# One contiguous tile of block-diagonal queries, loaded with its zeros in one DMA

## The chip, the cores and the metric

One core of a Trainium2 chip runs the whole program. The metric is device time in microseconds, from the first instruction to the end of the launch. The profile shows one execution of the same program.

## The reference, cut to what matters

A block-sparse attention is followed by two feed-forward layers. The part that the change touches is the scores:

```python
scores_l = scale * np.matmul(q, k.transpose(0, 1, 3, 2))       # masked to |i - j| < 16
k_sum = k.reshape(B, H, nb, 32, D).max(axis=3)                 # 24 blocks of 32 keys
scores_s = scale * np.einsum('bhsd,bhnd->bhsn', q, k_sum) + np.log(32)
a = softmax(concatenate([scores_l_m, scores_s], axis=-1))
x = matmul(a, concatenate([v, v_sum], axis=2))                 # -> (1536, 512)
h = x @ w_in;  x = (h - np.tanh(h)) @ w_out                    # d_ff 2048
xn = x / rms(x) * rms_g
out = (silu(xn @ w_gate) * (xn @ w_val)) @ w_out2              # d_ff 1536
```

There are 2 batches, 8 heads, 768 positions and a head dimension of 64, in float32. The feed-forward weights come as float64 and are split on the chip into pairs of float32r.

## The kernel before, in words

**Attention.** The positions of a batch are cut into six tiles of 128 queries (`TPB`). A unit `u` is one tile with four of the eight heads, so a batch has 12 units (u0 to u11, then u12 to u23). A head has only 64 rows of head dimension, so the 128 rows of TensorE hold two half-tiles of 64 queries at once: the stationary operand is block diagonal, with the first 64 queries in rows 0 to 63 and the second 64 in rows 64 to 127, and zeros in the two other quarters. The moving operand is the key window of both halves, 120 columns: 96 local keys and 24 block maxima.

The queries lie in three buffers `q0` to `q2` (`QB`). A buffer is `[128, 2, 64, 8]`, with the heads innermost, so the stationary operand of one head is every eighth float of the row. `zeros` (L168) clears the two zero quarters of each buffer once at the start, on GpSimd, and `qload` (L240) fills the two others with two DMAs of 64 rows each. `scores` (L258) does four matmuls for a unit (L271), VectorE adds the mask and takes the row extreme (L274), ScalarE takes the exponential (L276), VectorE and GpSimd normalise (L277 to L279). `trans` (L282) transposes the result (L286), and `pv` (L294) multiplies by the values (L303) and writes `xT`. The keys of a batch come in four tiles `kw` (L185). A key tile of the second batch takes the buffer of one of the first batch, when the last unit that reads it is through (u4, u5, u10, u11). `ksum_a` and `ksum_b` (L187 to L200) work out the block maxima and put them into the key tiles; two short matmuls each (L196) stand there with the contiguous tile `sel` as the stationary operand.

**Feed-forward.** `decode_next` (L129) loads a raw piece of a weight (L136, three raw buffers) and decodes it: L144 on ScalarE, L145 to L147 on VectorE, L152 on ScalarE or L150 on VectorE, L153 on GpSimd. The first layer starts while attention runs: an up step (`up1`, L315 to L317, 12 matmuls of 256 columns) and three steps later its down step (L350 to L352). Ten decoded pieces fit beside attention. Eight more get their place when the memory of attention is given back.

**Order.** A plan gives every task a due time (`task`, L428), the tasks are written out in that order, and the language's scheduler then places the instructions on each engine's queue by its own timeline. So an edit can move instructions that it does not touch. All DMAs are issued from one queue (SP), in order, and a DMA there waits until an earlier one has landed, eight places back.

Of the kernel before, what the change touches and what calls it, by code (L numbers as in the profile page):

```python
# [7 lines left out]
F32 = mybir.dt.float32  # L8
# [8 lines left out]
B, H, S, D = 2, 8, 768, 64  # L17
# [7 lines left out]
TPB = S // 128  # L25
KT = TPB // 2
LOC = 64 + 2 * WIN
WID = LOC + NB
# [7 lines left out]
QB = 3  # L36
# [9 lines left out]
DLD = 10  # L46
# [15 lines left out]
PTV = 0  # L62
KBUF = 4
PVS = (1, 1)
TQZ = 0.3
PB = 4
PTB = 3
SHIFT = {}
# [4 lines left out]
TQ = (0.2, 3)  # L73
# [10 lines left out]
def attn_moe_kernel(ctx: ExitStack, tc: tile.TileContext, ins, out, dbg=None):  # L84
    nc = tc.nc
    V, A, G, T = nc.vector, nc.scalar, nc.gpsimd, nc.tensor
# [13 lines left out]
    ap1 = att_ctx.enter_context(tc.tile_pool(name="ap1", bufs=1))  # L100
# [16 lines left out]
        nc.sync.dma_start(out=mask, in_=ins["mask"])  # L117
        nc.sync.dma_start(out=rg, in_=ins["rms_g"])

# [1 line left out]
    pieces = []  # L121
    for m in range(FF1 // 128):
        pieces += [("w_in", m), ("w_out", m)]
# [29 lines left out]
        G.tensor_tensor(w[:, 1], d, f(w[:, 0]), ALU.subtract)  # L153
        wt[name, m] = w

# [1 line left out]
    kwin, kmax, vsum, vt_ = {}, {}, {}, {}  # L157
    p_t, pt_t = {}, {}
    q_b = [ap1.tile([128, 2, 64, 8], F32, name=f"q{i}") for i in range(QB)]
    v_b = [ap1.tile([128, 2, DM], F32, name=f"v{i}") for i in range(VB)]  # L160
    v_of = {}
    xT = cst.tile([128, NT // 128, 2, KD, 128], F32R, name="xT")
# [1 line left out]

    def unit(u):
        return u // (2 * TPB), (u // 2) % TPB, u % 2

    def zeros(i):  # L168
        G.memset(q_b[i][0:64, 1], 0.0)
        G.memset(q_b[i][64:128, 0], 0.0)  # L170

    def ksum_a(b, par, hf):
        if not kwin:
# [65 lines left out]

    def qload(i):  # L240
        b, t = divmod(i, TPB)
        for s in range(2):
            nc.sync.dma_start(out=q_b[i % QB][s * 64:(s + 1) * 64, s].rearrange("p n k -> p (n k)"), in_=ins["q"][b, t, s])

    def vload(i):
        b, t = divmod(i, TPB)
# [3 lines left out]
    def vfill(i):  # L250
        b = i // TPB
        v = v_b[i % VB]
        if v_of.get(i % VB) != b:
            v_of[i % VB] = b
            for s in range(2):
                nc.sync.dma_start(out=v[LOC:WID, s], in_=vsum[b])

    def scores(u):  # L258
        b, t, par = unit(u)
        q = q_b[(u // 2) % QB].rearrange("p s n k -> p (s n) k")  # L260
        kw = kwin[b, par, t // KT][:, t % KT].rearrange("p (j k c) -> p j k c", j=5, k=4)
        mk = mask[:, 1 if 0 < t < TPB - 1 else (0 if t == 0 else 2)]
        P = Pp.tile([128, 4, WID], F32, name="P")
        nb = sp.tile([128, 4], F32, name="nb")
        sm = sp.tile([128, 4], F32, name="sm")
        nh = 2 if (u < S2) != (f"sh{u}" in ALT) else 4
        for k0 in range(0, 4, nh):
            ps = ps_h.tile([128, 512], F32, name="h") if u < SSH else ps_t.tile([128, 512], F32, name="t")
            for i in range(nh):
                k = k0 + i  # L270
                T.matmul(ps[:, i * WID:(i + 1) * WID], q[:, :, 4 * par + k], kw[:, :, k], start=True, stop=True)  # L271
            for i in range(nh):
                k = k0 + i
                V.tensor_tensor_reduce(P[:, k], ps[:, i * WID:(i + 1) * WID], mk, -0.125, 3e38, ALU.add, ALU.min, nb[:, k:k + 1])  # L274
        for k in range(4):
            A.activation(P[:, k], P[:, k], AF.Exp, scale=-1.0, bias=nb[:, k:k + 1], accum_out=sm[:, k:k + 1])  # L276
        V.tensor_scalar(sm, sm, 1e-9, None, ALU.add)  # L277
        V.reciprocal(sm, sm)
        (V if (u < PSV) != (f"ps{u}" in ALT) else G).tensor_tensor(P, P, sm.rearrange("p (k o) -> p k o", o=1).to_broadcast([128, 4, WID]), ALU.mult)  # L279
        p_t[u] = P  # L280

    def trans(u):  # L282
        P = p_t.pop(u)
        ps = ps_t.tile([128, 512], F32, name="t")
        for k in range(4):
            T.transpose(ps[0:WID, k * 128:(k + 1) * 128], P[:, k], ident)  # L286
        pt = ptp.tile([128, 512], F32, name="pt")
        if (u % 4 < PTV) != (f"pt{u}" in ALT):
            V.tensor_copy(pt[0:WID], ps[0:WID])
        else:  # L290
            A.activation(pt[0:WID], ps[0:WID], AF.Copy)
        pt_t[u] = pt
# [13 lines left out]
        A.activation(xh, ov, AF.Copy)  # L306
        V.tensor_tensor(xl, ov, f(xh), ALU.subtract)

# [1 line left out]
    def up(ps, w, t0, t1):  # L310
        o = ps[:, 0:(t1 - t0) * 128]
        for kk in range(KD):
            ws = slice(kk * 128, (kk + 1) * 128)
            xh, xl = xT[:, t0:t1, 0, kk], xT[:, t0:t1, 1, kk]
            T.matmul(o, w[:, 0, ws], xh, start=(kk == 0), stop=False)  # L315
            T.matmul(o, w[:, 1, ws], xh, start=False, stop=False)  # L316
            T.matmul(o, w[:, 0, ws], xl, start=False, stop=(kk == KD - 1))  # L317
# [37 lines left out]
    for md, chunks in enumerate((NCH, NCH2)):  # L355
        m0 = 0
        for j, nch in enumerate(chunks):
            t0 = 0
            pos = 2 * (j == len(chunks) - 1) + (j == 0)
            k = len(chunks) * 0 + (j if md == 0 else len(NCH) + j)  # L360
# [61 lines left out]
            A.activation(xh, pv, AF.Copy, scale=rg[:, kk:kk + 1])  # L422
            V.scalar_tensor_tensor(xl, pv, rg[:, kk:kk + 1], f(xh), ALU.mult, ALU.subtract)

# [1 line left out]
    plan = {}  # L426

    def task(key, at, fn, *req):  # L428
        plan[key] = (at + SHIFT.get(key, 0), len(plan), fn, req)
# [8 lines left out]
    def t_sc(u):  # L438
        u = ORD.index(u) if u < len(ORD) else u
        return TS0 + min(u, UF) * DT0 + max(u - UF, 0) * DT1  # L440

    for i in range(QB):
        task(f"z{i}", TQZ + i, lambda i=i: zeros(i))
    task("sel", TSEL, lambda: nc.sync.dma_start(out=sel, in_=ins["sel"]))
    task("cst", TC, consts)
    for par in range(2):
        at = TK01 * par
# [6 lines left out]
    at = t_sc(2 * TPB)  # L454
    for par in range(2):
        for hf in range(2):
            i = 2 * par + hf + 4 - KBUF
# [5 lines left out]
    for u in range(NU):  # L463
        b, t, par = unit(u)
        at = t_sc(u)
        i = u // 2
        if par == 0:
            task(f"ld{i}", TQ[i] if i < 2 else at - DLD, lambda i=i: qload(i), f"z{i % QB}", *([f"sc{2 * (i - QB) + 1}"] if i >= QB else []))
        task(f"sc{u}", at, lambda u=u: scores(u), f"ld{i}", f"kb{b}{par}", "cst")
        task(f"tr{u}", at + DTR, lambda u=u: trans(u), f"sc{u}")  # L470
        if par == 0:
            task(f"vf{i}", at + DPV - 2, lambda i=i: vfill(i), f"vs{b}", f"vl{i}")
            task(f"vl{i}", TVL[i] if i < 2 else at + DPV - DVL, lambda i=i: vload(i), *([f"pv{i - VB}"] if i >= VB else []))
        if par == 1:
            task(f"pv{i}", at + DPV, lambda i=i: pv(i), f"tr{u - 1}", f"tr{u}", f"vf{i}", *([f"pv{i - 1}"] if i else []))
# [4 lines left out]
    at = TM0  # L480
# [41 lines left out]
def layouts(q, k, v, moe_w_in, moe_w_out, moe2_w_gate, moe2_w_val, moe2_w_out, moe2_rms_g):  # L522
    import numpy as np

    def words(a):
        return np.ascontiguousarray(a).view(np.int64)

    def cols(w):
        n = w.shape[1] // 128
        return np.ascontiguousarray(words(w).reshape(KD, 128, n, 128).transpose(2, 1, 0, 3)).reshape(n, 128, 512)  # L530

    def rows(w):
        return words(w).reshape(w.shape[0] // 128, 128, DM)

    kp = np.zeros((B, H, S + 2 * WIN, D), np.float32)
    kp[:, :, WIN:WIN + S] = k
    vp = np.zeros((B, S + 2 * WIN, DM), np.float32)
    vt = v.transpose(0, 2, 1, 3).reshape(B, S, DM)
    vp[:, WIN:WIN + S] = vt
    order = np.r_[0:72, 80:96, 72:80]  # L540
    rows_at = (64 * np.arange(2 * TPB)[:, None] + order[None, :]).reshape(-1)
    qt = q.reshape(B, 4, 2, TPB, 2, 64, D).transpose(0, 3, 4, 6, 5, 2, 1)
    kw = kp[:, :, rows_at].reshape(B, 4, 2, TPB, 2, 4, 24, D).transpose(0, 2, 4, 7, 3, 5, 1, 6)
    vw = vp[:, rows_at].reshape(B, TPB, 2, LOC, DM).transpose(0, 1, 3, 2, 4)
    vs = v.reshape(B, 4, 2, TPB, 2, 2, BLK, D).transpose(0, 1, 2, 7, 4, 3, 5, 6).reshape(B, 4, 128, S)
    mask = np.zeros((128, 3, WID), np.float32)
    p, c = np.arange(128)[:, None], order[None, :]
    band = (c - p % 64 >= 1) & (c - p % 64 <= 2 * WIN - 1)
    for i in range(3):
        ok = band & ((c >= WIN) | (p >= 64) | (i != 0)) & ((c < 64 + WIN) | (p < 64) | (i != 2))  # L550
        mask[:, i, 0:LOC] = np.where(ok, 0.0, -8e9)
        mask[:, i, LOC:] = 8.0 * np.log(BLK)
    return {
        "q": np.ascontiguousarray(qt).reshape(B, TPB, 2, D, 512),
        "kw": np.ascontiguousarray(kw).reshape(B, 2, 128, TPB, 4 * LOC),
        "vt": np.ascontiguousarray(vs), "vw": np.ascontiguousarray(vw),
        "mask": mask,
        "sel": np.eye(128, dtype=np.float32).reshape(128, 2, 1, 64).repeat(2, axis=2).reshape(128, 256),
        "rms_g": np.ascontiguousarray(moe2_rms_g.reshape(KD, 128).T),
        "w_in": cols(moe_w_in), "w_out": rows(moe_w_out),  # L560
        "w_gate": cols(moe2_w_gate), "w_val": cols(moe2_w_val), "w_out2": rows(moe2_w_out),
    }
# [18 lines left out]
```

## Time and profile before

| | |
|---|---|
| time, three runs | 674.95, 675.65, 677.61 us; median 675.65 |
| span of the profiled execution | 673.4 us, so the median run lies 2.25 us above it |
| TensorE matmuls busy | 650.7 us, 97% |
| TensorE weight loads busy | 545.6 us, 81% |
| VectorE busy | 362.7 us, 54% |
| ScalarE busy | 262.5 us, 39% |
| GpSimd busy | 149.6 us, 22% |
| DMA | 55.71 MB, mean 83 GB/s |

The profile does not show the time of the profiled execution outside its span. PE is TensorE's matmuls, PEld its weight loads, DVE VectorE, ACT ScalarE, POOL GpSimd, SP the queue that issues DMAs. A float32 matmul that is not a transpose shows up as two pairs of a load and a matmul, so a unit of scores has eight records. Attention fills the span up to 142.3 us, with the first feed-forward layer beside it from 41 us on.

### The profile page before, as it was taken

To read this page: it belongs to the slowest core of one execution; us is meant where nothing else is said; L and a number is where in the kernel's file an instruction comes from. 1 tells how busy PE (TensorE), PEld (TensorE's weight loads), DVE (VectorE), ACT (ScalarE), POOL (GpSimd) and SP (SyncE) were. 2 spreads that over 40 slices of the span, in tenths; PEclk is the share of its full clock that TensorE was granted. 3 is DMA by queue.
4 is the path that set the end of the run, shared out by engine and by line. 5 is a ranking of instruction groups with operands and counts; after the bars stand their busy time and mean duration, and the time that the engine had idled before them with its cause. 6 is when DMAs were issued, how large, how long until landed. Compare 5 with 4: busy or idle time off the path is not lost.

```text
span 673.4 us, 8971 instructions
## 1 busy us (share of the span) xinstructions
PE 650.7 (97%) x3336; PEld 545.6 (81%) x3336; DVE 362.7 (54%) x780; ACT 262.5 (39%) x599; POOL 149.6 (22%) x171
## 2 busy tenths in 40 slices
PE   3988999999999999999999999999999999999997
PEld 3977999988778888888888888888888888888886
DVE  4898584469984387626577742222576611311312
ACT  1875775645542345325455332212445311111110
POOL 2558721124320123202052220001233200000000
PEclk9989999999999999999999999999999999999999
DMA  9978362004440024101023310000334000100101
GB/s 288 282 213 244 110 220 66 25 32 157 143 170 1 27 68 155 63 1 62 23 72 114 107 62 1 0 1 0 126 125 152 7 0 1 52 11 1 62 1 62
DMA packets 19827, 55.71 MB, mean 83 GB/s; under 512 B 2360, under 2 KB 5688, under 8 KB 19784
## 3 DMA queue, kind: packets, MB, share of 16 engines
q1 hardware_dynamic: 19784, 55.15, 25.2%
q8 instruction: 26, 0.43, 0.3%
q14 instruction: 17, 0.14, 0.1%
HBM read 51.70 MB, written 3.15 MB: 81 GB/s over the span
## 4 chain that ended last, share of the span: by engine, by line
PE 85%; DVE 8%; DMA 3%; issue 2%; SPq 1%; POOL 0%; ACT 0%; DVEq 0%; ACTq 0%; POOLq 0%
PE h L315 10%; PE h L316 10%; PE h L317 10%; PE acc L350 8%; PE acc L351 8%; PE acc L352 8%; PE t L317 5%; PE t L315 5%; PE t L316 5%; PE t L271 4%; DVE dt L146 2%; PE accx L352 2%; PE accx L351 2%; PE accx L350 2%; DMA kw<-kw 2%
## 5 line engine op out<-in xcount | busy, mean ns | idle before, releaser
L153 POOL TENSOR_TENSOR w<-dt,w 128x512 fp32r<-128x512 f32 x68 | 93.4, 1379 | 289.1 <-ACT w L152 277.0
L315 PE MATMUL h<-xT,w 128*128 128x512 f32 (+1 forms) x384 | 141.5, 369 | 2.1 <-DVE gt L325 2.0
L316 PE MATMUL h<-xT,w 128*128 128x512 f32 (+1 forms) x384 | 140.6, 366 | 0.0
L317 PE MATMUL h<-xT,w 128*128 128x512 f32 (+1 forms) x384 | 140.4, 366 | 0.0
L350 PE MATMUL acc<-w,g 128*128 128x512 f32 x264 | 104.7, 399 | 1.9 <-ACT g L333 1.8
L351 PE MATMUL acc<-w,g 128*128 128x512 f32 x264 | 103.8, 393 | 0.4 <-DVE g L334 0.4
L352 PE MATMUL acc<-w,g 128*128 128x512 f32 x264 | 103.7, 393 | 0.0
L333 ACT ACTIVATE g<-gt 128x512 fp32r<-128x512 f32 (+1 forms) x96 | 55.3, 577 | 112.3 <-DVE gt L345 85.3
L345 DVE TENSOR_TENSOR gt<-t,gt 128x512 f32<-128x512 f32 x36 | 24.8, 690 | 133.0 <-PE t L317 130.0
L315 PEld LDWEIGHTS h<-xT,w 128*128 128x128 f32 x384 | 72.5, 189 | 16.3 <-DVE gt L325 4.0
L316 PEld LDWEIGHTS h<-xT,w 128*128 128x128 f32 x384 | 72.7, 189 | 12.6
L317 PEld LDWEIGHTS h<-xT,w 128*128 128x128 f32 x384 | 72.4, 189 | 12.1
L334 DVE TENSOR_TENSOR g<-gt,g 128x512 fp32r<-128x512 f32 (+1 forms) x96 | 64.5, 673 | 32.7 <-ACT g L333 31.6
L144 ACT ACTIVATE da<-raw 128x512 f32<-128x512 f32 x68 | 45.4, 672 | 64.8 <-DVE dt L146 23.4
L350 PEld LDWEIGHTS acc<-w,g 128*128 128x128 f32 x264 | 49.4, 188 | 12.8 <-ACT g L333 2.1
L351 PEld LDWEIGHTS acc<-w,g 128*128 128x128 f32 x264 | 49.9, 189 | 10.9 <-DVE g L334 0.7
L352 PEld LDWEIGHTS acc<-w,g 128*128 128x128 f32 x264 | 49.6, 188 | 11.0
L147 DVE SCALAR_TENSOR_TENSOR dt<-raw,dt 128x512 uint32<-128x512 uint32 x68 | 57.7, 849 | 1.0
L145 DVE TENSOR_SCALAR dt<-raw 128x512 uint32<-128x512 uint32 x68 | 40.2, 591 | 32.0 <-POOL w L153 30.4
L325 DVE TENSOR_TENSOR gt<-h,gt 128x512 f32<-128x512 f32 (+1 forms) x60 | 34.6, 577 | 41.5 <-ACT gt L324 41.3
L317 PE MATMUL t<-xT,w 128*128 128x512 f32 x144 | 56.5, 392 | 0.0
L315 PE MATMUL t<-xT,w 128*128 128x512 f32 x144 | 56.4, 392 | 0.0
(83 smaller groups left out, 863.7 us busy)
## 6 DMA issues: line engine op xcount, KB each, us to landing
raw<-w_out SPq DMA_DIRECT2D x28, 512.0 KB, 3.3
raw<-w_in SPq DMA_DIRECT2D x16, 512.0 KB, 3.5
raw<-w_gate SPq DMA_DIRECT2D x12, 512.0 KB, 3.6
raw<-w_val SPq DMA_DIRECT2D x12, 512.0 KB, 3.2
kw<-kw SPq DMA_DIRECT2D x8, 576.0 KB, 4.9
v<-vw SPq DMA_DIRECT2D x12, 384.0 KB, 5.7
q<-q SPq DMA_DIRECT2D x24, 128.0 KB, 4.9
out_dram<-part SPq DMA_DIRECT2D x12, 256.0 KB, 2.1
```

The source lines that it names most:

```text
L144: A.activation(a, r[:, :, 1].bitcast(F32), AF.Copy, scale=2.0 ** -112)
L145: V.tensor_scalar(t, r[:, :, 0], 29, None, ALU.logical_shift_right)
L147: V.scalar_tensor_tensor(t, r[:, :, 1], 0x80000000, t, ALU.bitwise_and, ALU.bitwise_or)
L153: G.tensor_tensor(w[:, 1], d, f(w[:, 0]), ALU.subtract)
L315: T.matmul(o, w[:, 0, ws], xh, start=(kk == 0), stop=False)
L316: T.matmul(o, w[:, 1, ws], xh, start=False, stop=False)
L317: T.matmul(o, w[:, 0, ws], xl, start=False, stop=(kk == KD - 1))
L333: A.activation(g[:, 0, 0:n], t[:, 0:n], AF.Copy)
L334: V.tensor_tensor(g[:, 1, 0:n], t[:, 0:n], f(g[:, 0, 0:n]), ALU.subtract)
L350: T.matmul(o, g[:, 0, js], w[:, 0], start=first, stop=False)
L351: T.matmul(o, g[:, 1, js], w[:, 0], start=False, stop=False)
L352: T.matmul(o, g[:, 0, js], w[:, 1], start=False, stop=last)
```

## The change

The query buffer becomes `[128, 8, 128]`: for each head its 128 stationary columns lie side by side, zeros included. The host lays out the input so, with the zero quarters in it, and one DMA of 128 rows by 4 KB loads a tile, where two DMAs of 64 rows by 2 KB did. The GpSimd clears and their tasks are gone. Arithmetic and tile sizes on the chip stay as they were. The input `q` grows from 128 KB twice to 512 KB for a tile.

```diff
-    q_b = [ap1.tile([128, 2, 64, 8], F32, name=f"q{i}") for i in range(QB)]
+    q_b = [ap1.tile([128, 8, 128], F32, name=f"q{i}") for i in range(QB)]
...
-    def zeros(i):
-        G.memset(q_b[i][0:64, 1], 0.0)
-        G.memset(q_b[i][64:128, 0], 0.0)
...
     def qload(i):
         b, t = divmod(i, TPB)
-        for s in range(2):
-            nc.sync.dma_start(out=q_b[i % QB][s * 64:(s + 1) * 64, s].rearrange("p n k -> p (n k)"), in_=ins["q"][b, t, s])
+        nc.sync.dma_start(out=q_b[i % QB].rearrange("p k n -> p (k n)"), in_=ins["q"][b, t])
...
-        q = q_b[(u // 2) % QB].rearrange("p s n k -> p (s n) k")
+        q = q_b[(u // 2) % QB]
...
-                T.matmul(ps[:, i * WID:(i + 1) * WID], q[:, :, 4 * par + k], kw[:, :, k], start=True, stop=True)
+                T.matmul(ps[:, i * WID:(i + 1) * WID], q[:, 4 * par + k], kw[:, :, k], start=True, stop=True)
...
-    qt = q.reshape(B, 4, 2, TPB, 2, 64, D).transpose(0, 3, 4, 6, 5, 2, 1)
+    qt = q.reshape(B, 4, 2, TPB, 2, 64, D).transpose(0, 3, 4, 6, 2, 1, 5).reshape(B, TPB, 2, D, 8, 64)
+    qz = np.zeros((B, TPB, 2, D, 8, 2, 64), np.float32)
+    for s in range(2):
+        qz[:, :, s, :, :, s] = qt[:, :, s]
...
-        "q": np.ascontiguousarray(qt).reshape(B, TPB, 2, D, 512),
+        "q": qz.reshape(B, TPB, 128, 1024),
```

Line numbers of the changed kernel are smaller by 1 to 8. The scores (L271) are L265 there, the transposes (L286) L280, the products with the values (L303) L297, the short matmuls (L196) L191, the up step (L315 to L317) L309 to L311, the decode (L145 to L147) L144 to L146, the normalisation (L277, L278) L271 and L272, L325 is L319, L334 is L328, and L236 is L231.

The scheduler moves instructions on every engine up to about the end of attention; behind it the order is the same. Three places are shown. The first is the DMA queue at the start of the program. Before:

```order
L185 DMA kw<-kw 128x3x384
L243 DMA q_106<-q 64x512 x2
L185 DMA kw<-kw 128x3x384
L444 DMA sel<-sel 128x256
L117 DMA mask<-mask 128x360
```

and now:

```order
L180 DMA kw<-kw 128x3x384
L237 DMA q_106<-q 128x1024
L180 DMA kw<-kw 128x3x384
L436 DMA sel<-sel 128x256
L116 DMA mask<-mask 128x360
```

One DMA stands where two stood, and nothing else moves among the first twelve or so.

The second place is TensorE's queue just ahead of u12, the first unit of the second batch. The short matmuls with `mx` are those of `ksum_b`, `q_106` is the buffer that u12 reads. Before:

```order
L351 MATMUL acc<-w,g 128x512
L352 MATMUL acc<-w,g 128x512
L351 MATMUL acc<-w,g 128x512
L352 MATMUL acc<-w,g 128x512
L196 MATMUL t<-mx,sel 128x48 x2
L271 MATMUL t<-kw,q_106 128x120 x4
L286 MATMUL t<-sel,P 120x128 x4
L315 MATMUL h<-xT,w 128x256 x2
```

and now:

```order
L310 MATMUL h<-xT,w 128x256
L311 MATMUL h<-xT,w 128x256
L309 MATMUL h<-xT,w 128x256
L310 MATMUL h<-xT,w 128x256
L311 MATMUL h<-xT,w 128x256
L191 MATMUL t<-mx,sel 128x48 x2
L265 MATMUL t<-kw,q_106 128x120 x4
L280 MATMUL t<-sel,P 120x128 x4
```

An up step that followed u12 now precedes it: 49 matmuls of 256 columns stand ahead of u12, where 36 stood.

The third place is VectorE's queue between the score reductions of u15 and those of u16. `dt` and `raw` are of the weight decode. Before:

```order
L307 TENSOR_TENSOR xT<-acc,xT 128x512
L334 TENSOR_TENSOR g<-gt,g 128x256
L277 TENSOR_SCALAR sm<-sm 128x4
L278 RECIPROCAL sm<-sm 128x4
L325 TENSOR_TENSOR gt<-h,gt 128x256
L391 COPY part<-acc 128x512
L334 TENSOR_TENSOR g<-gt,g 128x256
L145 TENSOR_SCALAR dt<-raw 128x512
L325 TENSOR_TENSOR gt<-h,gt 128x256
L146 SCALAR_TENSOR_TENSOR dt<-da,dt 128x512
L147 SCALAR_TENSOR_TENSOR dt<-raw,dt 128x512
```

and now:

```order
L328 TENSOR_TENSOR g<-gt,g 128x256
L144 TENSOR_SCALAR dt<-raw 128x512
L145 SCALAR_TENSOR_TENSOR dt<-da,dt 128x512
L144 TENSOR_SCALAR dt<-raw 128x512
L271 TENSOR_SCALAR sm<-sm 128x4
L146 SCALAR_TENSOR_TENSOR dt<-raw,dt 128x512
L272 RECIPROCAL sm<-sm 128x4
L145 SCALAR_TENSOR_TENSOR dt<-da,dt 128x512
L319 TENSOR_TENSOR gt<-h,gt 128x256
L231 TENSOR_SCALAR vsum<-t 24x512
L146 SCALAR_TENSOR_TENSOR dt<-raw,dt 128x512
```

The decode of weight pieces has moved about a unit ahead of the scores. Between the last `ksum_b` copy (L198) and the end of u16, VectorE now has two more decodes of a piece (L145 to L147), the scaling of `vsum` (L236), one more L325 and one more L334. On TensorE, from the first matmul of u12 to the first of u16, there stand 48 matmuls of 256 columns as before, but 16 of 512 columns where there were 7, and four transposes of L224 where there were two.

## Rows read from the trace of the kernel before

**Rows 1.** The page: its first line.

```profile
span 673.4 us, 8971 instructions
```

**Rows 2.** The chain that ended last: start us, us, what.

```profile
54.28 7.09 DMA kw<-kw
...
68.69 0.12 PE h L315
...
127.27 1.90 PE t L271 x8
...
141.15 1.09 PE acc L303 x30
...
142.75 0.63 ACT w L152
...
196.91 0.61 DVE gt L325
```

**Rows 3.** Windows; busy us (instructions) of PE, PEld, DVE, ACT, POOL; clock, DMA share, GB/s.

```profile
14.00:64.90 50.90, 45.46 (x358) 41.77 (x359) 45.16 (x175) 35.27 (x124) 29.48 (x33) 0.97 0.89 258
...
36.00:46.00 10.00, 7.80 (x67) 7.63 (x68) 9.95 (x39) 6.62 (x22) 4.53 (x5) 0.83 0.70 194
...
56.00:66.00 10.00, 8.06 (x66) 6.20 (x64) 8.27 (x29) 5.76 (x16) 7.20 (x11) 1.00 0.89 251
...
64.90:85.80 20.90, 20.90 (x151) 20.23 (x151) 13.60 (x57) 13.86 (x49) 14.84 (x23) 1.00 0.41 133
...
64.90:142.30 77.40, 77.40 (x637) 72.32 (x637) 44.71 (x178) 47.07 (x159) 25.38 (x33) 1.00 0.30 98
...
142.30:200.00 57.70, 54.98 (x267) 44.48 (x268) 54.46 (x77) 31.11 (x59) 22.26 (x16) 1.00 0.40 138
```

**Rows 4.** Line L271: duration in ns (min/median/max), first and last start.

```profile
L271 PEld LDWEIGHTS t<-kw,q x128: 312/335/338, 38.6 to 128.6; 128*128 128x128 f32 x128
...
L271 PE MATMUL t<-kw,q x128: 267/402/498, 38.7 to 128.8; 128*128 128x120 f32 x128
```

**Rows 5.** Line L196, as above.

```profile
L196 PEld LDWEIGHTS t<-mx,sel x16: 186/240/338, 9.1 to 64.8; 128*128 128x128 f32 x16
```

**Rows 6.** Timeline of the weight loads around u12: start us, us, what.

```profile
64.45 0.52 PEld L196 LDWEIGHTS t<-mx,sel 128*128 128x128 f32 x4 [0.75 <-DVE mx L190]
...
64.89 1.98 PEld L271 LDWEIGHTS t<-kw,q 128*128 128x128 f32 x8
```

**Rows 7.** Timeline of TensorE, early; in brackets idle time before, and its releaser.

```profile
19.64 1.06 PE L286 MATMUL t<-sel,P 128*120 128x128 f32 x4
...
20.49 3.89 PE L271 MATMUL h<-kw,q 128*128 128x120 f32 x16
...
24.21 0.60 PE L286 MATMUL t<-sel,P 128*120 128x128 f32 x4
...
28.39 4.04 PE L271 MATMUL h<-kw,q 128*128 128x120 f32 x16 [0.66 <-DMA q<-q]
```

**Rows 8.** Timeline of the DMA queue: the first query load and the fourteenth.

```profile
1.24 1.19 SPq L243 DMA_DIRECT2D q<-q  x2
...
33.68 0.51 SPq L243 DMA_DIRECT2D q<-q  x1
```

**Rows 9.** DMA issues: count, size of each, median us to landing.

```profile
q<-q SPq DMA_DIRECT2D x24, 128.0 KB, 4.9
```

**Rows 10.** VectorE from 64.9 to 142.3 us: busy us, mean ns; idle before.

```profile
L325 DVE TENSOR_TENSOR gt<-h,gt 128x256 f32<-128x256 f32 x15 | 6.3, 417 | 9.4 <-ACT gt L324 9.2
...
L145 DVE TENSOR_SCALAR dt<-raw 128x512 uint32<-128x512 uint32 x5 | 3.1, 617 | 1.6 <-DMA raw<-w_in 1.0 <-DMA raw<-w_out 0.6
...
L146 DVE SCALAR_TENSOR_TENSOR dt<-da,dt 128x512 uint32<-128x512 uint32 x5 | 5.0, 1015 | 0.0
...
L147 DVE SCALAR_TENSOR_TENSOR dt<-raw,dt 128x512 uint32<-128x512 uint32 x5 | 3.5, 695 | 0.0
```

**Rows 11.** Timeline of GpSimd behind its clears.

```profile
10.62 0.34 POOL L199 COPY kw<-kw 128x192 f32<-128x192 f32 x1 [6.56 <-DVE kw L198]
```

More of the change, by code (lines that the diff above doesn't have):

```diff
@@ L64 @@
 PVS = (1, 1)
-TQZ = 0.3
 PB = 4
@@ L440, in t_sc @@
         return TS0 + min(u, UF) * DT0 + max(u - UF, 0) * DT1
-    for i in range(QB):
-        task(f"z{i}", TQZ + i, lambda i=i: zeros(i))
     task("sel", TSEL, lambda: nc.sync.dma_start(out=sel, in_=ins["sel"]))
@@ L467, in attn_moe_kernel @@
         if par == 0:
-            task(f"ld{i}", TQ[i] if i < 2 else at - DLD, lambda i=i: qload(i), f"z{i % QB}", *([f"sc{2 * (i - QB) + 1}"] if i >= QB else []))
+            task(f"ld{i}", TQ[i] if i < 2 else at - DLD, lambda i=i: qload(i), *([f"sc{2 * (i - QB) + 1}"] if i >= QB else []))
         task(f"sc{u}", at, lambda u=u: scores(u), f"ld{i}", f"kb{b}{par}", "cst")
```

## The prediction

> **What bounds the kernel now.** I read the chain of waits first, followed back from the last instruction. Behind 197 us it is TensorE alone. Between 142.75 and 197 us it runs through the decode of weights on VectorE, and that stretch opens when the last `pv` is through and attention gives its memory back: the step ahead of 142.75 is L303 on TensorE at 141.15 [rows 2]. The windows agree: from 142.3 to 200 us VectorE is busy for 54.46 of 57.7 us [rows 3]. So whatever moves the end of attention moves everything behind it, 531.1 us of the 673.4 [rows 1, 3], unchanged in work and in order.
>
> What sets the end of attention I read from the windows ahead of it. From 64.9 to 142.3 us TensorE has no idle time at all (77.40 of 77.40), while VectorE is busy for 44.71 and ScalarE for 47.07 us [rows 3]. That stretch begins with u12, and it is TensorE's. From 14 to 64.9 us no engine alone is the bound: VectorE is busy for 45.16 of 50.9 us, the DMA engines for 0.89 of the time at 258 GB/s, and the chain passes through a key tile that is issued when u11 is through and takes 7.09 us [rows 2, 3].
>
> Then the scores themselves. A unit's eight records take 1.90 us on the chain, 0.237 us each [rows 2]. Is that the matmul or the load of its weights? A matmul of L271 takes 267 ns at the least and 402 in the middle, with the same 120 columns and the same key tile [rows 4]: most of them wait for some 135 ns. The loads take 335 ns [rows 4]. The nearest loads of as many columns from a contiguous tile, L196, take 240 ns in the middle and 186 at the least [rows 5], and four of them stand 0.44 us apart from the next load, 0.110 us each, just ahead of u12 [rows 6]. So it is the load.
>
> **The rule on loads, and the row.** In rows, a load with 32 bytes between columns costs 0.237 us and one without a gap 0.110. The Trainium skill, TensorE: Matmul & The Clock Gate, section LDWEIGHTS (loading the stationary operand), has the time of a load depend on the number of columns alone; by that rule the new layout would load no faster and the sum below would lose its first term. SBUF — State Buffer, section Specifications (TRN2), says that memory is read in lines of 16 bytes and that fewer than two accesses to a line cost bandwidth; by that one the old layout, one float to a line, pays and the new one doesn't. The trace agrees with the second.
>
> **The change, part by part.**
>
> *Faster loads.* From u12 on there are 12 units of eight records, 96 of them. Each falls from 0.237 to 0.110 us if loads still set the pace. Ahead of that there is the matmul itself: its 267 ns against 402 say that it could follow 135 ns sooner, so 0.102 us apart [rows 2, 4], under 0.110. I take 0.127 us for each, 12.2 us. At the lower clock it would be little: the four transposes at 19.64 us take 0.85 us up to the next work, 0.213 each, and 1.06 with their end, those at 24.21 only 0.60 with their end [rows 7]. So TensorE was at the lower of its two levels, 1.2 GHz, up to somewhere between 20.5 and 24.2 us, and I take 22. The sixteen score records at 20.49 cross that point and need 0.233 us each all the same [rows 7]. The strided load does not care for the clock; a contiguous one does.
>
> *Moved matmuls.* Thirteen matmuls of 256 columns now stand ahead of u12 instead of behind it, 0.12 us each [rows 2]: 1.6 us out of the stretch in which TensorE is the bound, into one in which it isn't (8.06 of 10 us busy from 56 to 66 [rows 3], and with faster scores there it has more room). If there is no room they cost the same there, and the term is 0.
>
> *VectorE's decode moved ahead.* Up to the end of u16 VectorE gets two more decodes, 0.617 + 1.015 + 0.695 us each [rows 10], and three more short ones at some 0.42 [rows 10] (for L334 and the scaling of `vsum` that is an estimate from L325): 5.9 us. From 64.9 to 85.8 us, to the end of u16, it is busy for 13.60 [rows 3], so it would need 19.5. TensorE's own work there shrinks by 40 x 0.127 = 5.1 and grows by nine matmuls of 512 columns at 0.24 (an estimate, twice the 256) and two transposes at 0.11: 20.9 - 5.1 + 2.2 + 0.2 = 18.2. VectorE is short by 1.3 us without a gap, and it waits for raw pieces in between. Bounds: 0, if TensorE runs ahead of it by that much, to 5.9. I take 1.6 lost, near the lower end, since units are normalised long before they are transposed. What is late next are the up steps, which wait for VectorE to free the two `h` banks.
>
> *More bytes.* A tile grows by 256 KB. The DMA engines at full share move 258 / 0.89 = 290 GB/s early and 138 / 0.40 = 345 GB/s later [rows 3]: 0.90 or 0.76 us for a tile. Seven tiles are issued by 33.7 us (14 DMAs [rows 8, 9]), so 5.3 to 6.3 us of transfer in a stretch in which the engines have little room. Where it shows is the load that u6 waits for at 28.39 us [rows 7]: four tiles lie up to there, 3.0 to 3.6 us. Against it stand 0.6 us, the issue of a second DMA (two take 1.19 us [rows 8]), saved ahead of the first keys, and about 2 us that TensorE gains from 22 us on (the second half of the sixteen records at 20.49 and the eight behind them, 16 x 0.127). Net I take 0.7 us lost by the start of u12. Bounds: 5.7 lost (6.3 less the 0.6), to 5.7 gained, all that VectorE is idle from 14 to 64.9 us [rows 3]; nothing of it is likely at either end, since VectorE's work up to u12 is the same. Behind 65 us the DMA engines are at 0.30 [rows 3], and the bytes are hidden by that; at a share near 1 they would cost 0.8 us a tile.
>
> *The clears.* Six on GpSimd are gone. They end 6.56 us before GpSimd has its next work at 10.62 [rows 11]; that idle time hides them, and without it they would cost their 3 us.
>
> The sum: -12.2 - 1.6 + 1.6 + 0.7 = -11.5 us. The span goes from 673.4 to 661.9 us, and with the 2.25 us by which the median run lies above the span the time is **664.2 us**, 1.7% less.
>
> **The rivals.**
>
> *The early stage or VectorE takes most of it back.* If the extra bytes delay the raw pieces and the second batch's keys by the full 5, or VectorE's moved decodes cost TensorE their full 5.9 us, the gain is 13.8 less 5 or less 10: 4 to 9 us, 667 to 672. For it: VectorE is at 9.95 of 10 us from 36 to 46 [rows 3], and scores that come sooner don't make it faster. Against it: its idle 7.3 us from 64.9 to 85.8.
>
> *The early stage gives more.* If TensorE's faster scores let u11 finish earlier, the key tile behind it comes earlier and u12 with it, up to the 5.7 us: 657 to 660. Against it: VectorE is nearly full.
>
> *The change doesn't do what it says.* If the 0.237 us belong to the moving operand, which is read in pieces of 24 columns and stays as it is, loads get shorter in the trace and the pace stays: the 96 records gain nothing, 0.7 is lost, 675 to 677. L196, my model for the new load, has a contiguous moving operand of 48 columns as well, so it can't tell the two apart; the 267 ns of single L271 matmuls speak against it. The columns-alone rule of the Trainium skill's TensorE page comes out at the same place.
>
> *Slower: the clock falls.* TensorE fell to half its clock once, for 10 x 0.17 x 2 = 3.4 us in the window from 36 to 46 us (0.83) [rows 3], where it had just waited for a unit to transpose. If lighter scores leave holes like that from 65 us on, each spell costs half its length, 1.7 us; from nine spells on, 15 us, the gain of 13.8 is gone and the kernel is slower, say 680. Against it: the stretch has no idle time now, and from 142.3 to 200 us with 2.7 us idle the clock stays at 1.00 [rows 3].
>
> **How the numbers follow.** The forecast, 660 to 667 us, has 0.60; more than that (under 660) 0.14; most of it taken back (667 to 672.3) 0.18; no change by the pace 0.05; slower by the clock 0.03. What a measurement of this kernel can tell from no change is 0.5%, 3.4 us, so faster is under 672.3: 0.60 + 0.14 + 0.18 = 0.92. Same 0.05, slower 0.03. The range takes in the better case to 657 and most of the third to 670.5.
>
> **What would show it.** Right: L271's successor with loads near 190 to 240 ns, matmuls near 280, and eight records in 0.9 us from u12 on; the last `pv` ends near 131 us; behind it nothing but a shift. Wrong in the first term: the unit's piece on the chain stays near 1.9 us. Wrong in the early term: u12 starts far from 65.6 us. Wrong in the third: TensorE has idle time between u12 and the last `pv`, with VectorE as its releaser. The clock column below 1.00 there would mean the slower rival.

## The result and the profile after

The changed kernel takes **664.82 us** (median of 4 runs, 663.06 to 665.52), the kernel before 676.63 us beside it (674.95 to 678.25): a ratio of 0.9824, with an interval from 0.9805 to 0.9844. The profiled run took 664.97 us, with a span of 663.2 us, against 673.4 us in [rows 1]: 10.2 us less.

First the scores' own line in the changed kernel (L265 there, L271 before): duration in ns (min/median/max), first and last start. It answers to [rows 4].

```profile
L265 PEld LDWEIGHTS t<-kw,q x128: 186/192/337, 37.4 to 118.9; 128*128 128x128 f32 x128
L265 PE MATMUL t<-kw,q x128: 263/275/421, 37.6 to 119.0; 128*128 128x120 f32 x128
```

The load falls from 335 to 192 ns in the middle, and the matmul with it from 402 to 275, close to what only the quickest took before. The chain that ended last shows the same by units: eight records take 0.90 us here, and took 1.90 in [rows 2].

```profile
23.32 0.90 PE h L265 x8
...
99.39 0.88 PE t L265 x8
```

Then the windows, cut at the same events as [rows 3] (u12 starts at 67.10, the last `pv` ends at 132.3); columns as there: busy us (instructions) of PE, PEld, DVE, ACT, POOL, then clock, DMA share and GB/s.

```profile
14.00:67.10 53.10, 43.57 (x372) 38.66 (x371) 48.96 (x174) 35.37 (x125) 32.17 (x37) 0.87 0.89 288
36.00:46.00 10.00, 9.27 (x80) 8.76 (x81) 9.61 (x39) 7.45 (x30) 5.04 (x5) 0.70 0.78 205
46.00:56.00 10.00, 9.40 (x115) 8.15 (x114) 10.00 (x21) 6.11 (x19) 6.96 (x7) 1.00 0.71 229
56.00:67.10 11.10, 8.35 (x67) 6.74 (x65) 9.78 (x30) 5.66 (x17) 8.42 (x13) 0.85 0.84 265
67.10:132.40 65.30, 64.84 (x624) 58.85 (x624) 44.57 (x176) 45.42 (x158) 23.72 (x28) 1.00 0.37 121
132.40:190.10 57.70, 55.21 (x267) 44.80 (x268) 54.29 (x77) 31.23 (x59) 22.34 (x16) 1.00 0.42 138
```

The stretch from u12 to the last `pv` shrinks from 77.3 to 65.3 us, and TensorE fills it as before (64.84 of 65.30 us). It begins 2.2 us later, at 67.1 instead of 64.9. Behind it lie 530.9 us, which were 531.1: the rest of the kernel only moves ahead. So there are two things to explain, 12.0 us won behind u12 and 2.2 us lost ahead of it.

### The profile page after: what moved, and what is told of

The parts are those of the page before. It is cut to its first block, busy times and chain, and to the rows that moved or that the text cites. A ratio compares the mean times of both kernels' runs of the same rounds, so it can differ in the third digit from the quotient of the medians.

```text
span 663.2 us, 8941 instructions
## 1 busy us (share of the span) xinstructions
PE 636.4 (96%) x3336; PEld 529.2 (80%) x3336; DVE 366.5 (55%) x780; ACT 260.8 (39%) x599; POOL 147.7 (22%) x165
## 4 chain that ended last, share of the span: by engine, by line
PE 78%; DVE 13%; DMA 3%; issue 2%; POOL 1%; ACT 1%; SPq 0%; ACTq 0%; DVEq 0%; POOLq 0%
PE h L309 10%; PE h L311 10%; PE h L310 10%; PE acc L344 8%; PE acc L345 8%; PE acc L346 8%; PE t L311 5%; PE t L309 5%; PE t L310 5%; DVE dt L145 3%; DVE dt L146 2%; PE accx L346 2%; PE accx L345 2%; PE accx L344 2%; DVE dt L144 1%
## 5 line engine op out<-in xcount | busy, mean ns | idle before, releaser
L309 PE MATMUL h<-xT,w 128*128 128x512 f32 (+1 forms) x384 | 141.5, 369 | 1.9 <-DVE gt L319 1.7
L311 PE MATMUL h<-xT,w 128*128 128x512 f32 (+1 forms) x384 | 140.4, 366 | 0.0
L344 PE MATMUL acc<-w,g 128*128 128x512 f32 x264 | 105.0, 400 | 0.7 <-ACT g L327 0.5
L309 PEld LDWEIGHTS h<-xT,w 128*128 128x128 f32 x384 | 72.8, 190 | 16.1 <-DVE gt L319 3.6
L328 DVE TENSOR_TENSOR g<-gt,g 128x512 fp32r<-128x512 f32 (+1 forms) x96 | 66.1, 690 | 32.0 <-ACT g L327 30.9
L311 PEld LDWEIGHTS h<-xT,w 128*128 128x128 f32 x384 | 72.5, 189 | 12.4 <-DVE xT L301 0.2
L146 DVE SCALAR_TENSOR_TENSOR dt<-raw,dt 128x512 uint32<-128x512 uint32 x68 | 58.8, 866 | 1.1
L344 PEld LDWEIGHTS acc<-w,g 128*128 128x128 f32 x264 | 49.4, 188 | 12.0 <-ACT g L327 0.7
L319 DVE TENSOR_TENSOR gt<-h,gt 128x512 f32<-128x512 f32 (+1 forms) x60 | 34.7, 578 | 40.0 <-ACT gt L318 39.9
L145 DVE SCALAR_TENSOR_TENSOR dt<-da,dt 128x512 uint32<-128x512 uint32 x68 | 55.8, 822 | 1.7 <-ACT da L143 0.2
L311 PE MATMUL t<-xT,w 128*128 128x512 f32 x144 | 56.5, 392 | 0.0
L309 PE MATMUL t<-xT,w 128*128 128x512 f32 x144 | 56.4, 392 | 0.0
```

The source lines that it names most:

```text
L145: V.scalar_tensor_tensor(t, a.bitcast(U32), 3, t, ALU.logical_shift_left, ALU.bitwise_or)
L146: V.scalar_tensor_tensor(t, r[:, :, 1], 0x80000000, t, ALU.bitwise_and, ALU.bitwise_or)
L328: V.tensor_tensor(g[:, 1, 0:n], t[:, 0:n], f(g[:, 0, 0:n]), ALU.subtract)
L344: T.matmul(o, g[:, 0, js], w[:, 0], start=first, stop=False)
```

## Experiments

Each kernel was timed against the kernel before on the same chip. "u12", "the last pv" and "the stretch" between them are read from the trace of one profiled run, which is not always at the median: it took 2.9 us less in e4 and e6, 5.4 us more in e7, 2.1 more in e8, 1.9 more in e11, 1.6 more in e10, and up to 1.1 us from it in the others.

**e1, the old stride alone.** The changed kernel with everything it brings (zeros in the input, one DMA a tile, its order of instructions) but the heads innermost again, 32 bytes between a head's columns.

```
-    q_b = [ap1.tile([128, 8, 128], F32, name=f"q{i}") for i in range(QB)]
+    q_b = [ap1.tile([128, 128, 8], F32, name=f"q{i}") for i in range(QB)]
...
-                T.matmul(ps[:, i * WID:(i + 1) * WID], q[:, 4 * par + k], kw[:, :, k], start=True, stop=True)
+                T.matmul(ps[:, i * WID:(i + 1) * WID], q[:, :, 4 * par + k], kw[:, :, k], start=True, stop=True)
```

> The changed kernel with the heads innermost again (one float in eight), but zeros and the single DMA kept, and the order of all instructions as in the changed kernel. If the strided load is the cause, eight score records take 1.9 us again, the stretch from u12 to the last pv is 65.2 + 96 x 0.127 = 77.4 us, and the time is 664.8 + 12.2 = 677 us (675 to 679). If the new order or the single DMA made the gain, the time stays at 663 to 667 us, whatever the loads last.

Measured: 674.88 us, ratio 0.9989 (0.9972 to 1.0006), just under the 675 to 679 us expected. Loads and matmuls of the scores, in its trace:

```profile
L265 PEld LDWEIGHTS t<-kw,q x128: 312/335/338, 37.9 to 129.2; 128*128 128x128 f32 x128
L265 PE MATMUL t<-kw,q x128: 271/402/497, 38.1 to 129.3; 128*128 128x120 f32 x128
```

These are [rows 4] again to within a few ns. The instructions stand on every engine as in the changed kernel, the bytes are the same, only the address step differs, and the whole gain is gone. It is the stride of the stationary operand, not the order, the DMA or the clears. The run also measures the other parts of the change together: u12 starts at 66.51 us (1.6 later than before), the stretch takes 76.25 us (1.0 less), and the last `pv` ends at 142.76 us against 142.22: 0.5 us lost.

**e2 and e3, two strides between.** The heads in groups of two (8 bytes between columns) and of four (16 bytes), again with the instructions in the changed kernel's order.

```
-    q_b = [ap1.tile([128, 8, 128], F32, name=f"q{i}") for i in range(QB)]
+    q_b = [ap1.tile([128, 4, 128, 2], F32, name=f"q{i}") for i in range(QB)]
...
-                T.matmul(ps[:, i * WID:(i + 1) * WID], q[:, 4 * par + k], kw[:, :, k], start=True, stop=True)
+                T.matmul(ps[:, i * WID:(i + 1) * WID], q[:, (4 * par + k) // 2, :, (4 * par + k) % 2], kw[:, :, k], start=True, stop=True)
```

> The changed kernel with 8 bytes from one column to the next of the stationary operand (heads in pairs), all else equal. If a load pays for each line of 16 bytes that it uses only once, two columns lie in a line here, the pace stays 0.110 us and the time 665 us (663 to 667). If any gap between columns halves the pace, 0.237 us and 677 us.

> The changed kernel with 16 bytes from one column to the next (heads in fours), all else equal. If a line of 16 bytes that is used only once is what costs, the pace is 0.237 us as with 32 bytes, and the time 677 us (675 to 679). If the cost grows with the distance, it lies between: some 0.17 us and 671 us. If only 32 bytes cost, 0.110 us and 665 us.

Measured: 663.36 us with 8 bytes (ratio 0.9816, 0.9788 to 0.9843) and 674.56 us with 16 (0.9981, 0.9970 to 0.9993), again just under what was expected. The loads of e2, then of e3:

```profile
L265 PEld LDWEIGHTS t<-kw,q x128: 193/197/332, 36.9 to 118.6; 128*128 128x128 f32 x128
```

```profile
L265 PEld LDWEIGHTS t<-kw,q x128: 307/330/333, 37.5 to 128.2; 128*128 128x128 f32 x128
```

From one score record to the next it takes, in the middle, from u12 on, 0.112 us without a gap, 0.118 with 8 bytes, 0.233 with 16 and 0.238 with 32. The step lies between 8 and 16 bytes: two floats to a line of 16 bytes are all but free, one to a line costs what 32 bytes cost.

**e4, the layout without the zeros.** Contiguous heads, but cleared on GpSimd and loaded as two halves, with the bytes of before (two DMAs of 64 rows in pieces of 256 bytes).

```
-        nc.sync.dma_start(out=q_b[i % QB].rearrange("p k n -> p (k n)"), in_=ins["q"][b, t])
+        for s in range(2):
+            nc.sync.dma_start(out=q_b[i % QB][s * 64:(s + 1) * 64, :, s * 64:(s + 1) * 64], in_=ins["q"][b, t, s].rearrange("p (k n) -> p k n", k=8))
```

> Contiguous stationary operand, but the zeros cleared on GpSimd once and each tile loaded by two DMAs of 64 rows without the zeros, so with the bytes of before, in pieces of 256 bytes. The order is not that of the changed kernel. If the extra bytes cost the early stage, u12 starts before 67.1 us and the time is 661 to 664 us. If short pieces cost the DMA engines more than the bytes saved, u12 starts later, and the time is 666 to 670 us. In both the stretch from u12 to the last pv stays near 65 us.

Measured: 662.54 us, ratio 0.9803 (0.9770 to 0.9837). Loads take 192 ns in the middle, u12 starts at 62.99 us, and the stretch takes 64.5 us. The zeros and the single DMA are not needed for the gain. Two readings of the earlier u12 were left: the quarter of a megabyte a tile that isn't loaded, or the order, which comes out otherwise here.

**e5, the bytes in that order.** The changed kernel's tile and bytes by two DMAs of 64 rows; VectorE, TensorE and ScalarE have the order of e4.

```
+        for s in range(2):
+            r = slice(s * 64, s * 64 + 64)
+            nc.sync.dma_start(out=q_b[i % QB][r].rearrange("p k n -> p (k n)"), in_=ins["q"][b, t, r])
```

> The changed kernel's layout, zeros in the input and its bytes (512 KB a tile), but each tile by two DMAs of 64 rows, which gives every engine the order of the run with two half loads (e4), whose u12 began at 62.99 us and whose median was 662.54 us. If the 256 KB of zeros a tile are what made u12 late in the changed kernel (67.10 us): u12 near 67, 665 to 667 us. If it was the order in which the early work stands on VectorE: u12 near 63 to 63.5, 662 to 663 us.

Measured: 674.36 us, ratio 0.9970 (0.9943 to 0.9996), worse than either theory had it, though its loads are as short as those of the changed kernel and the stretch is 65.9 us. All of it is lost ahead of u12, which starts at 74.85 us. Its window up to u12, and the query tiles' DMAs from 14 to 60 us (count, size of each, median us to landing):

```profile
14.00:74.85 60.85, 41.72 (x371) 37.63 (x372) 44.64 (x178) 34.93 (x125) 29.93 (x35) 0.92 1.01 261
```

```profile
q<-q SPq DMA_DIRECT2D x11, 256.0 KB, 12.2
```

The same rows of the changed kernel and of e9 below:

```profile
q<-q SPq DMA_DIRECT2D x6, 512.0 KB, 8.2
```

```profile
q<-q SPq DMA_DIRECT2D x12, 256.0 KB, 7.7
```

Here the DMA engines are the bound: busy throughout (1.01), at 261 GB/s, while VectorE has 16 us of idle time. TensorE waits for pieces of the value tile and of queries.

**e6, the bytes twice.** The changed kernel with a second load of each tile into a tile that nothing reads.

```
         nc.sync.dma_start(out=q_b[i % QB].rearrange("p k n -> p (k n)"), in_=ins["q"][b, t])
+        nc.sync.dma_start(out=q_x, in_=ins["q"][b, t])
```

> The changed kernel with a second load of each tile (512 KB more, into a tile that nothing reads): the price of bytes at twice the dose. If the DMA engines bind the early stage, seven tiles at 1.5 to 1.8 us each (0.76 to 0.90 us per 256 KB) go through ahead of u12, of which the prediction would let 5 us or more reach it: u12 at 72 or later, 670 us or more. If the bytes go through at a higher rate behind VectorE's full stretch: u12 within 1.5 us of 67.1, 664 to 667 us.

Measured: 667.74 us (664.88 to 669.34), ratio 0.9858 (0.9823 to 0.9892). In its trace, that of its quickest run, u12 starts at 66.95 us, no later than in the changed kernel, though 15.5 MB instead of 13.7 go in between 14 and 60 us (its order is not quite the same). The time is just over the 664 to 667 us expected for that case.

```profile
14.00:66.95 52.95, 41.92 (x373) 37.44 (x373) 47.65 (x180) 35.50 (x128) 32.46 (x38) 0.90 1.04 332
```

The rate rises to 332 GB/s, and the DMA engines have no share left. The median is 2.9 us above the changed kernel's, with intervals that overlap. Six of the extra loads, not seven, are issued ahead of u12, and 22.0 MB have gone in by then, where the changed kernel has 19.6. These 2.4 MB more cost between 0 us, by the trace, and 3, by the medians, where the prediction's rates (290 to 345 GB/s) make it 7 to 8: in DMAs of 128 rows the bytes are not what holds u12.

**e9, two DMAs, all rows.** As e5, but each DMA takes four heads of all 128 rows, 2 KB a row. Its order is not quite that of e5.

```
+        for s in range(2):
+            nc.sync.dma_start(out=q_b[i % QB][:, 4 * s:4 * s + 4].rearrange("p k n -> p (k n)"), in_=ins["q"][b, t, :, 512 * s:512 * s + 512])
```

> The changed kernel with each tile by two DMAs that take all 128 rows, four heads each (2 KB a row), in place of the two DMAs of 64 rows of e5, whose u12 began at 74.85 us and whose packets of 4 KB took 251 ns between 20 and 36 us, against 165 in the changed kernel. If the 64 rows slow the transfers: u12 at 65 to 68 us, 663 to 667 us, and the packets of the decode's raw pieces back at 165 to 175 ns. If it is the second DMA that costs, or its order: u12 at 72 or later, 671 to 675 us.

Measured: 667.35 us, ratio 0.9859 (0.9833 to 0.9885); u12 at 66.87 us, and 292 GB/s up to there. So it is not the second DMA that costs in e5. Pieces of 4 KB a row are not it either, since the changed kernel has them too. What is left is that each DMA fills 64 rows; the order, which differs between e5 and e9, is not excluded by a run of its own. (The median is just over what was expected: its stretch takes 68.6 us, 2.3 of them a wait for the block sums' copy into the value tile.) The Trainium skill, SBUF — State Buffer, section Door 1: The DMA port swizzle (why [64,N] ≈ [32,N]), says that a transfer's bandwidth depends on the number of memory ports that its rows reach, and that rows 0 to 63 reach one half of them, 64 to 127 the other. The runs agree in the direction; which ports were busy they don't show.

**e7 and e8, VectorE ahead of u12.** e7 moves the first four casts of the decode to ScalarE (EV = 0). e8 moves the first eight subtractions from GpSimd to VectorE, and their casts to ScalarE:

```
+        A.activation(w[:, 0], d, AF.Copy)
+        (V if i < 8 else G).tensor_tensor(w[:, 1], d, f(w[:, 0]), ALU.subtract)
```

> The changed kernel with the first four casts of the decode on ScalarE in place of VectorE: 4 x 0.416 = 1.7 us less on VectorE ahead of u12. If VectorE binds the stretch before u12: u12 up to 1.7 us earlier, 662.5 to 664 us. If the bytes or the keys bind it: no earlier, 664 to 666 us. The order of the early work changes with it, so what VectorE's passes cost next to GpSimd's can move by as much either way.

> The changed kernel with the first eight subtractions of the decode on VectorE in place of GpSimd, and their casts on ScalarE. In the changed kernel a decode pass of VectorE takes 0.41 to 0.69 us alone and 0.95 to 1.8 us where GpSimd works at the same time. If the two engines hold each other up, the passes fall to their short times where GpSimd is idle, some 3 to 4 us less, against 8 x 0.68 - 1.7 = 3.7 us of work that VectorE takes over: u12 within 1.5 us of 67.1, 663 to 666 us, with the mean of the passes near 0.70 us (now 1.01, 0.85 and 0.66). If the long passes have another cause (the DMA's writes, say), their means stay and VectorE carries 3.7 us more: u12 near 70.8, 668 to 669 us.

Measured: e7 663.97 us (ratio 0.9821, 0.9774 to 0.9867), u12 at 65.1 us; e8 663.58 us (0.9791, 0.9747 to 0.9835), u12 at 63.2. VectorE's decode up to u12 in the changed kernel, and in e8 (busy us, mean ns):

```profile
L145 DVE SCALAR_TENSOR_TENSOR dt<-da,dt 128x512 uint32<-128x512 uint32 x7 | 7.1, 1011 | 0.1
L146 DVE SCALAR_TENSOR_TENSOR dt<-raw,dt 128x512 uint32<-128x512 uint32 x7 | 6.0, 852 | 0.0
L271 DVE TENSOR_SCALAR sm<-sm 128x4 f32<-128x4 f32 x12 | 5.5, 458 | 2.2 <-ACT P L270 2.2
L144 DVE TENSOR_SCALAR dt<-raw 128x512 uint32<-128x512 uint32 x8 | 5.3, 661 | 0.0
```

```profile
L145 DVE SCALAR_TENSOR_TENSOR dt<-da,dt 128x512 uint32<-128x512 uint32 x8 | 5.9, 733 | 0.1
L149 DVE TENSOR_TENSOR w<-dt,w 128x512 fp32r<-128x512 f32 x7 | 5.1, 724 | 0.1
L146 DVE SCALAR_TENSOR_TENSOR dt<-raw,dt 128x512 uint32<-128x512 uint32 x7 | 4.9, 713 | 0.0
L144 DVE TENSOR_SCALAR dt<-raw 128x512 uint32<-128x512 uint32 x8 | 4.1, 507 | 0.5 <-DMA raw<-w_out 0.5
```

VectorE does more in e8 and is done sooner: the passes fall by 0.14 to 0.28 us each where GpSimd isn't working beside them. That they get shorter was expected, that u12 starts 3.9 us earlier was not, since I had counted the new work as large as the saving. In e7 u12 comes 2.0 us earlier for 1.7 us of work taken away. The last key maxima (`mx`), which VectorE works out and the short matmuls ahead of u12 need, are ready at 65.25 us in the changed kernel, at 64.18 in e7 and at 62.63 in e8. Both runs speak for VectorE as a part of what set u12's start in the changed kernel, with a reserve: the order of the early work changes with each move. Neither run is faster for it, by the intervals: the stretch grows to 71.1 us in e7 (in a trace 5.4 us above its median, so the usual stretch may be shorter) and to 69.9 in e8, of which TensorE in e8 waits for this:

```profile
PE acc L294 <- DMA v<-vsum: 3.3, 1, 3.3
PE t L216 <- POOL vt L208: 1.2, 1, 1.2
```

**e10, that wait moved.** e8 with the second batch's block sums planned 3 steps earlier (TV1 = -11).

> The run with the subtractions on VectorE (e8), with the four loads and sums of the second batch's block sums planned 3 steps earlier. In e8 u12 began at 63.23 us, but the stretch from there to the last pv took 69.9 us in place of 65.3, of which TensorE waited 3.3 us for the sums' copy into the value tile and 1.2 for the sums themselves. If that wait is what took e8's gain back: it is gone or under 1 us, the stretch is 65 to 67 us, 659 to 662 us. If something else ends later there: the stretch stays near 70 us, 663 to 665 us.

Measured: 662.23 us, ratio 0.9795 (0.9772 to 0.9818). The wait is gone and the stretch is 63.9 us, less than the 65 expected, but u12 is back at 67.3 us: the sums now stand ahead of it, and TensorE waits there, 3.4 us for GpSimd's normalising and 2.3 for a cast on ScalarE. The time is above the 662 us that were expected at most. It is the lowest median of all kernels (by the ratio e8 is as low), but its interval overlaps that of the changed kernel: the two are not told apart, and no version that is surely better came out.

**e11, e4 with e8's move.** The layout of e4 and the subtractions of e8.

> The contiguous layout with the halves loaded apart and cleared on GpSimd (e4), with the first eight subtractions of the decode on VectorE and their casts on ScalarE (as e8). If VectorE and GpSimd holding each other up is what remains of the early stage: u12 at 61 to 63 us (62.99 in e4). If e4 already had the short passes, since its GpSimd work fell elsewhere: u12 no earlier than 63, 662 to 664 us, as e4.

Measured: 665.50 us, ratio 0.9834 (0.9808 to 0.9859), u12 at 71.7 us. Neither reading holds. The move doesn't help where the transfers bind: its DMAs of 64 rows take 8.3 us to land (6.4 in e4), and TensorE waits for them:

```profile
PE h L268 <- DMA q<-q: 5.4, 3, 2.8
PE acc L300 <- DMA v<-vw: 2.8, 1, 2.8
```

Why the same transfers went through in time in e4 and not here is left open; the order differs.

## Why the prediction was right, and which term was off

**What bounds it** held. The rest of the kernel moved by the end of attention: the last `pv` ends at 132.34 us (131 was named), 9.9 us earlier, and the span is 10.2 us shorter, where 11.5 were put. That the time came so close, 664.82 us for 664.2, is in part luck: the span is 1.3 us longer than forecast (663.2 for 661.9), but the median run lies only 1.6 us above it, where 2.25 were added.

**Faster loads: -12.2 put, -11.9 measured.** Summed by the distance from record to record, the 96 records took 22.66 us before and take 10.74 now. The pace is 0.112 us, the 0.110 that L196's contiguous loads had given [rows 6]. e1 to e3 show the cause, and settle what the prediction could only weigh. By the rule of columns alone (the Trainium skill, TensorE: Matmul & The Clock Gate, section LDWEIGHTS (loading the stationary operand)) e1 would have been as fast as the changed kernel. The rule of 16-byte lines, with two accesses to a line wanted (the Trainium skill, SBUF — State Buffer, section Specifications (TRN2)), puts the step where e2 and e3 have it.

**Moved matmuls: -1.6 put, -1.6 behind u12 by count.** Thirteen fewer of them stand there, 167 where 180 stood; in e1 their lines take 1.5 us less. Ahead of u12 they were to find room. In e1 they do, in the changed kernel they don't, as the lines under *More bytes* show.

**VectorE's decode: +1.6 put, about +1.5 left over**, but not in the form described. TensorE's idle time behind u12 is 0.46 us, of which one wait for VectorE shows:

```profile
PE acc L297 <- DVE xT L301: 0.3, 1, 0.3
```

The rest is records that stand a little farther apart (L309, 256 columns, 131 ns in the mean against 124 before; the transposes 103 against 98). What causes that was not tried, so that this term came out near its size is luck. The three terms together are -12.2 as put, and the stretch lost 12.0.

**More bytes: +0.7 put, +2.2 measured.** This is the mis-sized term, and just ahead of u12 nothing waits for bytes. u12 waits for two things, the last key maxima (`mx`) on VectorE and TensorE's own queue. The lines are from the kernel before, the changed kernel and e1, which has the same order as the changed kernel:

```profile
63.48 0.92 DVE L190 TENSOR_TENSOR mx<-m,m 128x24 f32<-128x24 f32 x1
64.45 0.65 PE L196 MATMUL t<-mx,sel 128*128 128x48 f32 x4 [0.32 <-DVE mx L190]
```

```profile
61.97 0.85 PE L344 MATMUL acc<-w,g 128*128 128x512 f32 x2
64.27 0.98 DVE L185 TENSOR_TENSOR mx<-m,m 128x24 f32<-128x24 f32 x1
66.72 0.54 PE L191 MATMUL t<-mx,sel 128*128 128x48 f32 x4
```

```profile
62.67 0.73 PE L344 MATMUL acc<-w,g 128*128 128x512 f32 x2
64.98 0.99 DVE L185 TENSOR_TENSOR mx<-m,m 128x24 f32<-128x24 f32 x1
66.04 0.63 PE L191 MATMUL t<-mx,sel 128*128 128x48 f32 x4
```

Before, TensorE waited for the maxima, ready at 64.40 us. In the changed kernel they are ready at 65.25, 0.85 us later, but the short matmuls start 1.5 us behind that: TensorE works without a gap up to u12, and the thirteen moved matmuls stand just there. From the first L344 of these lines to u12 it takes 5.13 us, and 3.84 in e1 for the same instructions. The 1.3 us between them are the clock, which is at the lower of its two levels from 62.4 to 65.8 us in the changed kernel and at 1.00 in e1 (e2 and e3, in the same order too, differ in the same way: 4.90 us at the lower clock and 3.83). The two windows, columns as in [rows 3]:

```profile
62.40:65.80 3.40, 3.40 (x12) 2.68 (x11) 3.40 (x8) 1.01 (x2) 2.78 (x5) 0.50 0.85 241
```

```profile
56.00:66.51 10.51, 9.30 (x79) 7.63 (x78) 10.48 (x30) 6.34 (x20) 8.99 (x14) 1.00 0.92 295
```

So some 0.85 of the 2.2 us came by VectorE, and 1.3 by TensorE's own queue at the lower clock, with the moved matmuls in it, for which the prediction had counted on room. In e1 they end as the maxima come (65.97 us), and cost nothing.

Two steps of the term itself failed. The price of bytes was wrong: I took 0.76 to 0.90 us for each 256 KB, at the rates of the kernel before. But with DMAs of 128 rows the rate is higher (343 GB/s in the first 36 us against 287, at shares of 0.98 and 0.99), and e6 adds 2.4 MB for 0 to 3 us. The other step that failed is "VectorE's work up to u12 is the same". In number it nearly is (174 instructions for 175, among them one more subtraction of `xT` and one more L144, 1.3 us); in time VectorE is busy for 48.96 us up to u12, against 45.16 in [rows 3], and for 49.22 in e1, so it is the order and not the faster scores. Most of the rest is operations that are longer where the new order puts GpSimd's work beside them. Of the twelve L271, the five with GpSimd idle take 0.16 to 0.17 us and the seven beside its work 0.36 to 0.96; before, two of twelve (L277) took so long. The two lines that grew most, before (they are L145 and L271 in the rows at e8, with 1011 and 458 ns in the mean):

```profile
L146 DVE SCALAR_TENSOR_TENSOR dt<-da,dt 128x512 uint32<-128x512 uint32 x7 | 5.7, 809 | 0.0
L277 DVE TENSOR_SCALAR sm<-sm 128x4 f32<-128x4 f32 x12 | 3.1, 261 | 0.0
```

Examples, from the timelines of VectorE and then of GpSimd in the changed kernel:

```profile
44.53 0.16 DVE L271 TENSOR_SCALAR sm<-sm 128x4 f32<-128x4 f32 x1
45.14 1.80 DVE L145 SCALAR_TENSOR_TENSOR dt<-da,dt 128x512 uint32<-128x512 uint32 x1
46.98 0.69 DVE L146 SCALAR_TENSOR_TENSOR dt<-raw,dt 128x512 uint32<-128x512 uint32 x1
47.59 0.95 DVE L271 TENSOR_SCALAR sm<-sm 128x4 f32<-128x4 f32 x1
```

```profile
45.10 1.30 POOL L152 TENSOR_TENSOR w<-dt,w 128x512 fp32r<-128x512 f32 x1 [2.58 <-DVE w L149]
47.20 1.31 POOL L273 TENSOR_TENSOR P<-P,sm 128x480 f32<-128x480 f32 x1 [0.81 <-ACT gt L318]
```

The four-element L271 takes 0.16 us with GpSimd idle, and 0.95 in the midst of a GpSimd multiplication, ending at 48.54 us, just behind it (48.51); L145 takes 1.80 us where it starts with a subtraction, 0.54 of them behind its end, and 0.69 with GpSimd idle. e8, where GpSimd's subtractions are gone, bears it out. The Trainium skill, SBUF — State Buffer, section Terms, names what would do this: the two engines share a pair of ports that one of them holds for a whole instruction. The ends agree with that; the ports themselves no run shows.

**The clears** cost nothing that shows: e1, without them but with the zeros' bytes, is within the measurement of the kernel before. The two were not tried apart.

**The rivals.** "The change doesn't do what it says" falls with the first rows. "Slower: the clock falls" came in part: the clock did fall, but ahead of u12: 0.87 from 14 to 67.1 us, so 53.1 x 0.13 x 2 = 13.8 us at the lower of its two levels, where [rows 3] has 0.97. Of that only the last spell is priced here, 1.3 us; what the earlier ones cost stays open. TensorE is idle up to u12 for 9.5 us, where it was for 5.4 before and is for 5.2 in e1 (0.97); but e9 has 12.9 us of idle time and 0.97, so idle time alone doesn't explain it. Behind u12 the clock is 1.00. "The early stage or VectorE takes most of it back" was the right place, with 2.2 us of its 5; in e5 it happened in full.

## What to carry to other kernels

Look at the address step of every stationary operand before anything else: with fp32, 16 or 32 bytes from one column to the next doubled the time from load to load, 8 bytes cost 5%, and no engine's busy share tells it, only loads and matmuls that are longer than the same shape elsewhere. When such a rewrite adds bytes, let each DMA fill all 128 rows: the same bytes in DMAs of 64 rows lost the whole gain (e5), though half the bytes in DMAs of 64 rows kept it (e4). And where one stage gets faster, read the next bound's operations for their lengths beside a neighbour engine's work, not only for their number.

## What the runs showed of the hardware that was not expected

- **The rate goes with the rows of a DMA.** From 14 us to u12 all transfers together ran at 261 GB/s with the DMA engines always busy where the queries came by 256 KB on 64 rows (e5), at 292 by 256 KB on 128 rows (e9), and at 288 (changed kernel) to 332 (e6) by 512 KB on 128 rows. Packets of 4 KB took 251 ns each in e5 and 165 in the changed kernel, in the middle, from 20 to 36 us.
- **A strided load does not care for the clock.** Without a gap a load takes 192 ns in the middle and up to 337, the long ones in the early stretch where the clock was low; with 16 or 32 bytes it is 330 to 336 ns in the middle at either level.
- **GpSimd holds up even the smallest VectorE operation**: four elements a row, 0.16 us alone, 0.95 us beside a GpSimd instruction of 1.31.
